# Spreading the first expert's scaling over later groups, with six matmuls of zeros at the start

## The chip, the cores and the metric

The kernel runs on one core of a Trainium2 chip. A core has five engines that run their own instruction streams and meet at semaphores: TensorE (PE, matmuls; its weight loads are shown apart as PEld), VectorE (DVE), ScalarE (ACT), GpSimd (POOL) and SyncE (SP, which only issues DMA transfers here). SBUF is the working memory; matmuls write to PSUM, which has eight banks of 512 fp32 numbers on each of 128 partitions. The metric is the device time of one execution in microseconds, the median over several runs.

## The reference

Attention with feature maps on 8 batches x 8 heads of 576 x 64 gives x of 4608 x 512; behind it stands a mixture of eight experts whose routing weights P are balanced by eight rounds of normalization:

```python
kv  = einsum('bhsf,bhsd->bhfd', phi(k), v);  z = phi(k).sum(axis=2)
x   = (phi(q) @ kv) / (phi(q) . z + 1e-06)      # as 4608 x 512
P   = exp(x @ w_gate - max)                     # 4608 x 8
for _ in range(8):
    P /= P.sum(1, keepdims=True) + 1e-09
    P /= P.sum(0, keepdims=True) + 1e-09
    P *= N / E
for e in range(8):
    h = maximum(x @ w1[e], 0.0)                 # 512 -> 1024
    out += P[:, e:e + 1] * (h @ w2[e])          # 1024 -> 512
```

## The kernel before

The attention stage fills xT, a bf16 copy of x with the feature dimension on the partitions. The tokens stand in nine groups of 512 (g = 0 to 8), and each group has an fp32 accumulator acc[g] of 128 x 4 x 512 in SBUF.

Expert 0 starts while the routing weights are still being formed. Its second products (`down0`) are therefore copied from PSUM to acc[g] without P, by ScalarE (L795) and VectorE (L802) in turn, and P[:, 0] is put on later: at the head of each group's work for expert 1, `down7` lets ScalarE multiply acc[g] in place, in four instructions of 128 x 512 (L1240). That makes 36 of these scalings.

Experts 1 to 7 use a scheme with seven products instead of eight on half-size blocks. `up7` forms a group's hidden values: TensorE adds products up in a bank (x1 to x4 in bank x, one after another), ScalarE copies intermediate states of it to fp32 buffers U (L1106, `keep`), VectorE adds them to other banks and clips at zero (L1110), and ScalarE writes the last state with a relu (L1115). x2 goes into the bank that x1 wrote, so TensorE can go on there only when ScalarE has copied it; the same holds for x3 and x4. `down7` forms sums S of hidden blocks on VectorE (L986) and the seven products X1 to X4, Y1, Z1, Z2. Their states go to acc[g] in two ways: VectorE multiplies by P and adds (L1218), or ScalarE multiplies by P into a buffer V (L1230) and GpSimd adds V to acc[g] (L1233). There are four U buffers and two V buffers. The second products of a group are interleaved with the first products of the next by a list of names (`ORDER`); the first group of expert 1 has none to be interleaved with.

The code doesn't fix the engines' order itself. Each operation is entered in a `Plan` with an engine, a duration that the code supposes, and keys it reads and writes. `schedule` then takes, again and again, the operation that can start first by these durations (of those that can start together, the one entered first), and the program is written out in that order. A key orders operations in the plan alone. On the chip an instruction waits at semaphores only for the data that it reads or overwrites, and for its place in its engine's queue. A scaling is entered with the planner's duration of 512/1200 + 0.09 = 0.52 us.

At the start, SP loads the first keys and queries into accumulators that aren't in use yet, TensorE transposes them (L545), VectorE and ScalarE copy the transposes (L549, L553), and TensorE multiplies by the feature weights wphi2 (L468), which VectorE has cleared (L818) and filled from two loads (L820).

Of the kernel before, what the change touches and what calls it, by code (L numbers as in the profile page):

```python
# [228 lines left out]
def kernel(  # L229
# [11 lines left out]
    nc = tc.nc  # L241
# [26 lines left out]
    xT = const.tile([128, NP, N], BF16, name="xT")  # L268
    L = const.tile([128, NT, E], FP32, name="L")
    P = const.tile([128, NT, E], FP32, name="P")  # L270

    NA = 5
    acc = [accp.tile([128, 4, DD], FP32, name=f"acc{g}", tag=f"acc{g}") for g in range(NA)]
# [17 lines left out]
    def pe(cols, fn, r=(), w=(), takes=()):  # L291
        plan.op("PE", max(cols / 2400.0 + 0.0025, 0.032), 0.32, fn, r, w, takes)

    def act(el, fn, r=(), w=()):
        plan.op("ACT", el / 1200.0 + 0.09, 0.22, fn, r, w)

    def dve(el, fn, r=(), w=(), shared=False):
        plan.op("DVE", el / 960.0 + 0.09, 0.22, fn, r, w, shared=shared)
# [4 lines left out]
    def dma(queue, nbytes, rate, fn, r=(), w=()):  # L303

        plan.op(queue, 0.8 if queue == "POOL" else 0.6, 0.0, fn, r, w, (), nbytes / rate / (125 / 100))
# [45 lines left out]
    def new(tag):  # L351
        return banks.new(int(tag[1])) if tag in ("P1", "P2") else R[tag].new()
# [29 lines left out]
    def load_qk(b, hh, nh, t, r=()):  # L382

        o = hh % 4
        keys = [o // 2] if nh == 2 else [0, 1]
        if b < 2:
            g = t["f"]
            for x, src in ((1, k), (0, q)):
                i = 2 * x + o // 2
                dma("SP", nh << 17, 268, lambda x=x, src=src, i=i: nc.sync.dma_start(  # L390
                    out=acc[g][:, i:i + nh // 2].rearrange("p a (h c) -> p (a h) c", h=2),
                    in_=src[b, hh:hh + nh, 0:SM].rearrange("h (p j) d -> p h (j d)", j=NJ)),
                    r, [("acc", g, 2 * x + n) for n in keys])
            return
        for x, src in ((1, k), (0, q)):
            dma("POOL", nh << 17, 200, lambda x=x, src=src: nc.gpsimd.dma_start(
                out=t["qk"]()[:, x, o:o + nh],
                in_=src[b, hh:hh + nh, 0:SM].rearrange("h (p j) d -> p h (j d)", j=NJ)),
                r, [(t["qk"], x, i) for i in keys])
# [25 lines left out]
    def new_half(b, i):  # L425

        t = {"T": new("qkT"), "v": new("v_m")}
        if b < 2:
            return {"f": 4 - 2 * b - i, **t}
        return {"qk": new("qk"), **t}  # L430
# [36 lines left out]
    def mm(out_, lhsT, rhs, start, stop):  # L467
        nc.tensor.matmul(out_, lhsT=lhsT, rhs=rhs, start=start, stop=stop)  # L468
# [310 lines left out]
    def akey(g):  # L779
        return ["late"] * (g >= NA) + ["P"] * (g >= 9)  # L780
# [27 lines left out]
    for b in range(2):  # L808
        for i in range(2):
            halves[b, i] = new_half(b, i)  # L810
    load_qk(0, 0, 2, halves[0, 0])
    for i, (queue, eng) in enumerate((("ACT", nc.scalar), ("POOL", nc.gpsimd))):
        dma(queue, 1 << 15, 100, lambda i=i, eng=eng: eng.dma_start(
            out=wphi_f[64 * i:64 * i + 64, :], in_=w_phi), w=[f"wphi_f{i}"])
# [16 lines left out]
    for i in range(2):  # L831
        for x in range(2):
            dve(300, lambda i=i, x=x: nc.vector.memset(vrd[i][x], 0.0),
                w=[("vrd", i, x, h, *y) for h in range(2) for y in ((), (1,))])
# [338 lines left out]
    def down7(e, g, hT, B7):  # L1173
# [64 lines left out]
        if e == 1 and g < 9:  # L1238
            for ts in range(4):
                act(512, lambda ts=ts: nc.scalar.activation(  # L1240
                    out=acc[g][:, ts, :], in_=acc[g][:, ts, :], func=ACT.Copy, bias=0.0,
                    scale=P[:, 4 * g + ts, 0:1]), ["P", ("acc", g, ts)] + akey(g),
                    [("acc", g, ts, j) for j in range(2)])
        x, y, z = new("P1"), new("P1"), new("P1")

# [38 lines left out]
    for e in range(1, E):  # L1284
        w1, w2 = load_w(e, ["late"])
        if e == 1:
            for g in range(NG):
                sums_x(g)
        A7, B7 = sums_w(e, w1, w2)
        for g in (range(NG) if e < E - 1 else [8, *range(8)]):  # L1290
            X = load_x(g)
            hT = [new("hT") for _ in range(2)]
            un = up7(A7, g, X, hT, ["up0"])
            for n in ORDER:
                if len(n) == 3:
                    un[n[:2], int(n[2])]()
                elif dn is not None:
                    dn[n]()
            if dn is not None:
                dn["out"]()  # L1300
            if e == E - 1 and g == 7:
                down8(e, g, hT, w2)
            else:
                dn = down7(e, g, hT, B7)
# [31 lines left out]
```

## Time and profile before

| | |
|---|---|
| median of 3 runs | 1036.96 us (1035.57 to 1037.59) |
| profiled execution | 1036.16 us, of which the span is 1034.4 us |
| TensorE busy | 1013.8 us (98%), 9476 matmuls |
| VectorE busy | 823.7 us (80%) |
| ScalarE busy | 710.9 us (69%) |
| GpSimd busy | 462.8 us (45%) |
| L1240, the 36 scalings | 24.3 us busy, on the chain of waits with 2% of the span |

Busy time is the union of an engine's instructions. A matmul's row shows its own length, 0.273 us for 256 columns, while the next one starts 0.11 us after it, so the ends overlap. Stages lie in the order of time: attention with expert 0's first groups beside it to about 205 us, expert 0 alone to about 254 us, experts 1 to 7 from there to the end.

### The profile page before, as it was taken

Reading aid. Unit: us, or ns where it says so; the run is one execution under the profiler, and the core shown is the slowest. Engines: PE = TensorE matmul, PEld = TensorE weight load, DVE = VectorE, ACT = ScalarE, POOL = GpSimd, SP = SyncE. Lnnn points to the kernel's source line nnn. Section 1 sums busy time; section 2 is a strip of 40 time slices with the busy share of each in tenths; the row PEclk is TensorE's granted clock in tenths of the full one; section 3 lists DMA queues with packets and bytes.
Section 4 is the critical chain, followed back from the end, with each engine's and each line's share of the span. In section 5 each row is a group of like instructions: output and inputs, shape, how many; then the busy total and the mean of one; then the engine's idle time right before and its main releaser. Section 6 shows DMA issues by size and latency. Waiting matters only on the chain.

```text
span 1034.4 us, 24481 instructions
## 1 busy us (share of the span) xinstructions
PE 1013.8 (98%) x9476; PEld 843.0 (81%) x9512; DVE 823.7 (80%) x1626; ACT 710.9 (69%) x1569; POOL 462.8 (45%) x534
## 2 busy tenths in 40 slices
PE   7899999999999999999999999999999999999998
PEld 5666666645788888888888888888888888888886
DVE  7999998987677788778777787788677877786775
ACT  7999999837966666666666656666666566666653
POOL 5877675400243443434443444434444433334442
PEclk9999999999999999999999999999999999999999
DMA  9998996085311161115211341134111611114333
GB/s 261 175 172 145 174 162 103 2 206 140 83 42 52 46 120 41 42 46 100 73 44 50 82 83 42 42 83 92 33 52 44 131 43 42 42 51 124 123 123 123
DMA packets 105237, 93.93 MB, mean 91 GB/s; under 512 B 45392, under 2 KB 80272, under 8 KB 105120
## 3 DMA queue, kind: packets, MB, share of 16 engines
q1 hardware_dynamic: 71360, 68.44, 24.3%
q0 software_dynamic: 33680, 23.90, 16.5%
q8 instruction: 74, 1.21, 0.5%
q14 instruction: 43, 0.35, 0.1%
q10 hardware_dynamic: 80, 0.03, 0.0%
HBM read 94.98 MB, written 14.16 MB: 106 GB/s over the span
## 4 chain that ended last, share of the span: by engine, by line
PE 92%; ACT 4%; DVE 3%; issue 1%; DMA 0%; DVEq 0%; POOLq 0%
PE P L1078 73%; PE P L468 17%; ACT acc L1240 2%; PE P L667 1%; DVE m L460 1%; ACT k L464 1%; PE P L706 1%; ACT q L464 0%; DMA wphi_f<-in_w_phi_dram 0%; DVE xb L687 0%; ACT U L1106 0%; DVE P L679 0%; PE P L672 0%; DVE S L986 0%; DVE m_r L460 0%
## 5 line engine op out<-in xcount | busy, mean ns | idle before, releaser
L1233 POOL TENSOR_TENSOR acc<-acc,V 128x512 f32<-128x512 f32 x248 | 316.1, 1281 | 440.5 <-ACT V L1230 437.6
L1110 DVE CUSTOM_DVE_ANT_0 hT<-P,U 128x512 bf16<-128x512 f32 x378 | 255.1, 687 | 105.9 <-ACT U L1106 56.7
L1106 ACT COPY U<-P 128x512 f32<-128x512 f32 x378 | 217.9, 590 | 139.0 <-PE P L1078 131.0
L1230 ACT ACTIVATE V<-P 128x256 f32<-128x256 f32 x496 | 205.6, 474 | 124.4 <-PE P L1078 119.2
L1218 DVE SCALAR_TENSOR_TENSOR acc<-P,acc 128x256 f32<-128x256 f32 x372 | 160.0, 478 | 73.7 <-PE P L1078 71.6
L1078 PEld LDWEIGHTS <-w 128*128 128x128 bf16 x2016 | 197.2, 98 | 25.2 <-issue 2.0
L1078 PEld LDWEIGHTS <-S 128*128 128x128 bf16 x1984 | 194.2, 98 | 22.4
L1078 PEld LDWEIGHTS <-T 128*128 128x128 bf16 x1512 | 147.9, 98 | 19.7 <-issue 2.5
L1078 PEld LDWEIGHTS <-hT 128*128 128x128 bf16 x1488 | 145.5, 98 | 17.1 <-DVE hT L1110 0.3
L1078 PE MATMUL P<-X,w 128*128 128x256 bf16 x1008 | 154.9, 273 | 0.4 <-ACT U L1106 0.4
L1078 PE MATMUL P<-xT,w 128*128 128x256 bf16 x1008 | 152.5, 273 | 0.9 <-ACT acc L795 0.5
L1078 PE MATMUL P<-X,T 128*128 128x256 bf16 x1008 | 148.6, 273 | 1.5 <-ACT U L1106 1.5
L1078 PE MATMUL P<-w,hT 128*128 128x256 bf16 x992 | 143.4, 273 | 0.0
L1078 PE MATMUL P<-T,S 128*128 128x256 bf16 x1056 | 136.3, 273 | 0.0
L1078 PE MATMUL P<-w,S 128*128 128x256 bf16 x928 | 126.5, 273 | 0.0
L460 DVE TENSOR_REDUCE m<-P 128x4 f32<-128x512 f32 x128 | 83.7, 679 | 3.4 <-PE P L468 2.1
L593 POOL TENSOR_TENSOR v<-v_m,em 128x512 bf16<-128x512 f32 x64 | 67.0, 1046 | 43.1 <-ACT em L464 39.0
L986 DVE TENSOR_TENSOR S<-hT 128x1024 bf16<-128x1024 bf16 x124 | 83.4, 709 | 0.3 <-ACT hT L1115 0.3
L1115 ACT ACTIVATE hT<-P 128x512 bf16<-128x512 f32 x126 | 74.2, 604 | 12.4 <-PE P L1078 11.9
L468 PE MATMUL P<-w,hT 128*128 128x512 bf16 x303 | 77.1, 379 | 0.9 <-DVE m L460 0.2
L1078 PE MATMUL P<-xT,T 128*128 128x256 bf16 x504 | 76.0, 273 | 0.3
L468 PE MATMUL P<-xT,w 128*128 128x512 bf16 x271 | 71.4, 379 | 1.0 <-ACT q L464 0.3
(95 smaller groups left out, 1096.5 us busy)
## 6 DMA issues: line engine op xcount, KB each, us to landing
X<-xd SPq DMA_DIRECT2D x126, 256.0 KB, 2.6
w<-in_moe_w_dram POOLq DMA_DIRECT2D x14, 1024.0 KB, 10.1
v_m<-in_v_dram SPq DMA_DIRECT2D x14, 512.0 KB, 5.2
out_dram<-acc SPq DMA_DIRECT2D x14, 512.0 KB, 2.7
xd<-S SPq DMA_DIRECT2D x18, 256.0 KB, 2.4
qk<-in_k_dram POOLq DMA_DIRECT2D x12, 256.0 KB, 5.5
qk<-in_q_dram POOLq DMA_DIRECT2D x12, 256.0 KB, 6.5
w<-in_moe_w_dram POOLq DMA_DIRECT2D x8, 256.0 KB, 7.7
```

What stands on the lines that cost most here:

```text
L460: dve(el, lambda: nc.vector.tensor_reduce(out=dst(), in_=src(), axis=AX.X, op=ALU.max, apply_absolute_value=True), r, w)
L468: nc.tensor.matmul(out_, lhsT=lhsT, rhs=rhs, start=start, stop=stop)
L593: pool(512, lambda y=y, em=em: nc.gpsimd.tensor_tensor(out=s["v"][y]()[:, :, 0:D], in0=t["v"]()[:, h0:h0 + 2].rearrange("p a (b c) -> p (a ...
L986: lambda: f.tensor_tensor(out=out_(), in0=x(), in1=y(), op=op), r, w, **kw)
L1078: pe(256, lambda i=i, k=k, z=z: nc.tensor.matmul(bank()[:, 256 * i:256 * i + 256], lhsT=lhs(k, i), rhs=rhs(k), start=first and z, stop=k = ...
L1106: act(512, lambda: nc.scalar.copy(out=u[fp][n]().rearrange("p a b -> p (a b)"), in_=x[fp]()), [x[fp]], [u[fp][n]])
L1110: dve(500, lambda: nc.vector._custom_dve(ADD_SAT, out=out_(fp, i, j), in0=bank[fp]().rearrange("p (a b) -> p a b", a=2), in1=u[fp][n](), s ...
L1115: act(512, lambda: nc.scalar.activation(out=out_(fp, i, j), in_=x[fp]().rearrange("p (a b) -> p a b", a=2), func=ACT.Relu, bias=0.0, scale ...
L1218: dve(330, lambda n=n, ts=ts: nc.vector.scalar_tensor_tensor(out=acc[g][:, ts, 256 * j:256 * j + 256], in0=bank()[:, 256 * n:256 * n + 256 ...
L1230: act(390, lambda n=n: nc.scalar.activation(out=u()[:, n, :], in_=bank()[:, 256 * n:256 * n + 256], func=ACT.Copy, bias=0.0, scale=P[:, 4 ...
L1233: pool(670, lambda: nc.gpsimd.tensor_tensor(out=acc[g][:, 2 * i:2 * i + 2, 256 * j:256 * j + 256], in0=acc[g][:, 2 * i:2 * i + 2, 256 * j: ...
L1240: act(512, lambda ts=ts: nc.scalar.activation(out=acc[g][:, ts, :], in_=acc[g][:, ts, :], func=ACT.Copy, bias=0.0, scale=P[:, 4 * g + ts, ...
```

## The change

Two edits. The first enters, ahead of the first loads of wphi, a clearing of 512 numbers of xT on VectorE and six products of 128 x 512 zeros on TensorE into a PSUM bank that nobody reads. They read nothing but the cleared part of xT, which the attention stage writes over later.

The second adds a key to the scalings of groups 2 to 8: the planner counts such a scaling as ready only when the last entered operation that wrote a part of acc of the group two ahead (the GpSimd add behind Y1) has ended by its times.

```diff
     load_qk(0, 0, 2, halves[0, 0])
+    dve(128, lambda: nc.vector.memset(xT[:, 0, 0:512], 0.0), w=[("xT", 0, 0)])
+    pz = new("P1")
+    for i in range(6):
+        pe(1024, lambda: mm(pz(), xT[:, 0, 0:128], xT[:, 0, 0:512], True, True),
+           [("xT", 0, 0)], [pz])
...
             for ts in range(4):
                 act(512, lambda ts=ts: nc.scalar.activation(
                     out=acc[g][:, ts, :], in_=acc[g][:, ts, :], func=ACT.Copy, bias=0.0,
-                    scale=P[:, 4 * g + ts, 0:1]), ["P", ("acc", g, ts)] + akey(g),
+                    scale=P[:, 4 * g + ts, 0:1]), ["P", ("acc", g, ts)] + akey(g)
+                    + ([("acc", g - 2, 0, 0)] if g >= 2 else []),
                     [("acc", g, ts, j) for j in range(2)])
```

Lines behind the first edit move by five, behind the second by six: L1240 becomes L1245, L1106 L1111, L1115 L1120, L1230 L1235, L820 L825.

The first place is ScalarE's queue where expert 0 ends and expert 1's first group begins. Before, with the waits at semaphores in brackets; acc_77 to acc_81 are acc[0] to acc[4], acc_4252 and up are acc[5] and up:

```order
L795 ACTIVATE acc_4254<-P 128x512 [waits PE_49]
L1240 ACTIVATE acc_78<-acc_78,P 128x512 x3
L1240 ACTIVATE acc_79<-acc_79,P 128x512 x3
L795 ACTIVATE acc_4255<-P 128x512 [waits PE_49]
L1240 ACTIVATE acc_79<-acc_79,P 128x512
L1240 ACTIVATE acc_80<-acc_80,P 128x512 x4
L1240 ACTIVATE acc_81<-acc_81,P 128x512
L795 ACTIVATE acc_4255<-P 128x512 [waits PE_49]
L1106 COPY U<-P 128x512 [waits PE_49,Pool_49]
L1106 COPY U<-P 128x512 [waits PE_49]
L1240 ACTIVATE acc_81<-acc_81,P 128x512
```

The same place of the changed kernel, where acc_4259 and up are acc[5] and up:

```order
L795 ACTIVATE acc_4261<-P 128x512 [waits PE_49]
L1245 ACTIVATE acc_78<-acc_78,P 128x512 x3
L795 ACTIVATE acc_4262<-P 128x512 [waits PE_49] x2
L1111 COPY U<-P 128x512 [waits PE_49,Pool_49]
L1111 COPY U<-P 128x512 [waits PE_49] x3
L1111 COPY U<-P 128x512 [waits DVE_49,PE_49] x2
L1120 ACTIVATE hT<-P 128x2x256 [waits PE_49] x2
L1235 ACTIVATE V<-P 128x256 [waits DVE_49,PE_49]
```

The scalings of acc[2] and up have left this place; behind those of acc[1] ScalarE's queue goes straight to the copies out of PSUM.

The second place is ScalarE's queue some four groups later. Before, it holds no scalings any more:

```order
L1106 COPY U<-P 128x512 [waits DVE_49,PE_49]
L1115 ACTIVATE hT<-P 128x2x256 [waits PE_49]
L1230 ACTIVATE V<-P 128x256 [waits PE_49,Pool_49]
L1230 ACTIVATE V<-P 128x256
L1115 ACTIVATE hT<-P 128x2x256 [waits PE_49]
```

In the changed kernel those of acc[4] stand there:

```order
L1111 COPY U<-P 128x512 [waits DVE_49,PE_49] x2
L1245 ACTIVATE acc_81<-acc_81,P 128x512
L1235 ACTIVATE V<-P 128x256 [waits PE_49,Pool_49]
L1235 ACTIVATE V<-P 128x256
L1120 ACTIVATE hT<-P 128x2x256 [waits PE_49] x2
L1245 ACTIVATE acc_81<-acc_81,P 128x512 x3
L1111 COPY U<-P 128x512 [waits DVE_49,PE_49] x2
```

One scaling has come ahead of the group's last V copies and three stand between its two relus and the next group's first U copies; none of them has a wait of its own.

The third place is VectorE's queue at the start of the program, before:

```order
L818 MEMSET wphi_88 128x128
L833 MEMSET vrd_89 128x520
L833 MEMSET vrd_90 128x520
L833 MEMSET vrd_91 128x520
L833 MEMSET vrd_92 128x520
L835 MEMSET colw 128x128
L820 CAST wphi_88<-wphi_f 64x128 x2
L549 CAST qkT<-P 128x512
```

and in the changed kernel (128x256 are four-byte words, two numbers each):

```order
L812 MEMSET xT 128x256
L823 MEMSET wphi_88 128x128
L838 MEMSET vrd_89 128x520
L838 MEMSET vrd_90 128x520
L838 MEMSET vrd_91 128x520
L838 MEMSET vrd_92 128x520
L840 MEMSET colw 128x128
L825 CAST wphi_88<-wphi_f 64x128 x2
```

One memset has come ahead of all others; what follows it is the same. TensorE's queue begins with the six pairs of a weight load and a matmul on xT and goes on as before up to expert 1.

## The prediction

> **What bounds the kernel now.** I read the page's busy times and its chain of waits first, then the table by stretches of time, then TensorE's own timeline at the stretch where the table shows a loss.
>
> ```profile
> PE 1013.8 (98%) x9476; PEld 843.0 (81%) x9512; DVE 823.7 (80%) x1626; ACT 710.9 (69%) x1569; POOL 462.8 (45%) x534
> PE 92%; ACT 4%; DVE 3%; issue 1%; DMA 0%; DVEq 0%; POOLq 0%
> L1240 ACT ACTIVATE acc<-acc,P x36: 706/740/885, 243.4 to 278.3; 128x512 f32<-128x512 f32 x36
> ```
>
> TensorE is busy for 98% of the span and carries 92% of the chain, so time can only be gained where it stands still. The third line (the scaling line alone: shortest, median and longest in ns, first and last start) says that the 36 scalings which the change spreads out all start within 35 us. The table by stretches shows what that does; its columns are the stretch, its length, then busy time and instructions of TensorE, weight loads, VectorE, ScalarE and GpSimd, the granted clock, and DMA.
>
> ```profile
> 255.00:260.00 5.00, 4.48 (x41) 3.77 (x39) 3.08 (x5) 5.00 (x11) 0.45 (x1) 1.00 0.78 104
> 260.00:265.00 5.00, 4.02 (x31) 2.72 (x29) 3.65 (x6) 5.00 (x11) 0.00 (x0) 1.00 0.95 215
> 265.00:270.00 5.00, 3.50 (x32) 2.83 (x30) 2.99 (x5) 5.00 (x11) 0.65 (x1) 1.00 0.00 1
> 270.00:275.00 5.00, 5.00 (x48) 4.50 (x46) 2.33 (x5) 5.00 (x12) 2.73 (x3) 1.00 0.19 52
> 275.00:280.00 5.00, 5.00 (x48) 4.41 (x47) 4.87 (x10) 5.00 (x10) 1.71 (x2) 1.00 0.22 56
> 300.00:400.00 100.00, 100.00 (x919) 89.62 (x917) 79.14 (x138) 61.95 (x130) 43.38 (x35) 1.00 0.29 67
> ```
>
> From 255 to 270 us ScalarE is busy without a pause and TensorE gets 41, 31 and 32 matmuls into stretches that hold 48 from 270 on. At the steady pace (100 us for 919, 0.109 us each) the 7 + 17 + 16 = 40 missing ones are worth 4.35 us. That is all there is to gain at this place: from 300 to 400 us TensorE is busy for 100.00 of 100 us. Who stops it there is in the timelines, of TensorE and then of ScalarE (start, length, what, and in brackets the idle time before and what ended it):
>
> ```profile
> 256.42 0.60 PE L1078 MATMUL P<-xT,w 128*128 128x256 bf16 x4 [0.52 <-ACT acc L795]
> 261.75 0.60 PE L1078 MATMUL P<-X,w 128*128 128x256 bf16 x4 [0.38 <-ACT U L1106]
> 264.68 0.60 PE L1078 MATMUL P<-xT,w 128*128 128x256 bf16 x4 [0.33 <-DVE hT L1110]
> 267.48 0.60 PE L1078 MATMUL P<-X,T 128*128 128x256 bf16 x4 [1.33 <-ACT U L1106]
> 268.58 0.60 PE L1078 MATMUL P<-X,T 128*128 128x256 bf16 x4 [0.17 <-ACT U L1106]
> ...
> 252.11 3.78 ACT L1240 ACTIVATE acc<-acc,P 128x512 f32<-128x512 f32 x6
> 255.79 0.59 ACT L795 ACTIVATE acc<-P 128x512 f32<-128x512 f32 x1
> 263.15 3.81 ACT L1240 ACTIVATE acc<-acc,P 128x512 f32<-128x512 f32 x6
> 266.82 0.61 ACT L1106 COPY U<-P 128x512 f32<-128x512 f32 x1
> ```
>
> Four of the five waits end with a ScalarE copy out of PSUM (L795, L1106), and the two longest of these copies stand right behind six scalings in a row, 3.78 and 3.81 us long. Those copies are what TensorE needs; the scalings are not needed until GpSimd and VectorE add to the same rows of acc.
>
> **The scaling, part by part.** The order in front of this text shows that from the third group on the scalings leave this place: behind the first eight, ScalarE now goes straight to two L795 copies and six U copies. Twenty-eight scalings move to later groups; their number and size don't change.
>
> What comes back at 255 to 270 us: at most 4.35 us. Not all of it, for the third wait above ends with VectorE, and expert 1's first group has no second products of an earlier group to fill TensorE while its own last sums are formed.
>
> ```profile
> L1110 DVE CUSTOM_DVE_ANT_0 hT<-P,U 128x512 bf16<-128x512 f32 x378 | 255.1, 687 | 105.9 <-ACT U L1106 56.7 <-PE P L1078 47.2
> L1078 PE MATMUL P<-X,w 128*128 128x256 bf16 x1008 | 154.9, 273 | 0.4 <-ACT U L1106 0.4
> ```
>
> The next to be late there is therefore the last product's end and its add, 0.27 + 0.69 = 0.96 us, before the first product that reads hT. I take this as uncovered once: 4.35 - 0.96 = 3.4 us gained. The ends are 4.35 (something fills it) and 1.83 (only what stands behind the second row of six comes back: 1.33 + 0.17 of idle time, and twice the 0.273 - 0.109 = 0.164 us by which a matmul's modelled end hides a stop).
>
> What the 28 scalings cost where they go: per group of 12 us, four scalings of 0.63 us (3.78 / 6) are 2.5 us, and ScalarE's share rises from 62% to about 83%. The nearest row on the good side is 270 to 280 us in the table: ScalarE is full in both stretches, seven of the scalings start there (the row below and four more in ones and twos), and TensorE still gets its 48. The nearest on the bad side is the second row of six, 1.83 us lost, 0.31 per scaling, or 28 x 0.31 = 8.5 us.
>
> ```profile
> 275.95 2.10 ACT L1240 ACTIVATE acc<-acc,P 128x512 f32<-128x512 f32 x3
> ```
>
> After the change no row of scalings that stands behind the first eight is longer than three, so the good row is the nearer one: I take 0. The gate itself costs nothing on the chip. It is an entry of the planner, the scaling reads nothing of the group two ahead, and in the built program these scalings carry no wait on GpSimd. Nothing can queue behind a gate that isn't there; what counts is only where they stand in ScalarE's order. GpSimd's and VectorE's adds to a group's acc wait for its scaling, but in the new order each stands at least four V copies ahead of that group's first. SP's order is the same row for row; GpSimd's has a weight load one add earlier or later in three places.
>
> **The six matmuls of zeros.** These are rows of the start: TensorE's, one of the table by stretches, VectorE's, and two of the chain of waits (start, length, what):
>
> ```profile
> 3.58 2.13 PE L545 MATMUL P<-identf,acc 128*128 128x128 f32 x8 [3.58 <-DMA acc<-in_k_dram]
> 6.15 1.89 PE L468 MATMUL P<-wphi,qkT 128*128 128x256 bf16 x8 [0.43 <-DVE qkT L549]
> 7.83 1.06 PE L468 MATMUL P<-qkT,wphi 128*128 128x512 bf16 x2
> 8.68 1.81 PE L545 MATMUL P<-identf,acc 128*128 128x128 f32 x8
> 12.36 0.61 PE L468 MATMUL P<-wphi,rT 128*128 128x256 bf16 x4 [0.42 <-DVE rT L485]
> 12.80 0.38 PE L468 MATMUL P<-rT,wphi 128*128 128x512 bf16 x1
> ...
> 6.00:10.00 4.00, 3.85 (x17) 2.90 (x18) 2.91 (x6) 3.11 (x9) 0.05 (x1) 1.00 1.18 203
> ...
> 0.83 0.17 DVE L818 MEMSET wphi<- 128x128 uint32 x1 [0.83 <-PEq L1320]
> 1.05 2.14 DVE L833 MEMSET vrd<- 128x520 bf16 x4
> 3.17 0.17 DVE L835 MEMSET colw<- 128x128 f32 x1
> 3.76 0.22 DVE L820 CAST wphi<-wphi_f 64x128 bf16<-64x128 f32 x1 [0.42 <-DMA wphi_f<-in_w_phi_dram]
> 5.14 0.22 DVE L820 CAST wphi<-wphi_f 64x128 bf16<-64x128 f32 x1 [1.16 <-DMA wphi_f<-in_w_phi_dram]
> 5.40 0.69 DVE L549 CAST qkT<-P 128x512 bf16<-128x512 f32 x1
> ...
> 6.15 1.05 PE P L468 x4
> 7.22 2.06 ACT k L464 x4
> ```
>
> The memset of 512 numbers lies between 0.17 us (128 four-byte words) and 0.54 (2.14 / 4, 520 bf16); say 0.3. VectorE's row then ends at 3.6 to 3.9 instead of 3.34 and the first cast waits for its load until 3.76; the second, at 5.14, is the one that counts and isn't moved. The zeros can start at about 1.2. Two 512-column products take 0.85 us here (7.83 to 8.68), so six take 2.55 and end near 3.75, 0.17 us behind the first transpose's old start. Its result isn't read before 5.40, so that too is covered; if it were not, it would cost 0.17.
>
> What they could give is the pace. Eight 256-column products at 6.15 take 1.68 us to issue (0.21 each), four at 12.36 take 0.44 (0.11 each): TensorE starts at half pace, though the clock column gives 1.00 from 6 to 10 us too. If it were at full pace by 6.15, the four products of the chain at 6.15 would end 4 x 0.10 = 0.4 us earlier, and ScalarE, which the chain follows from 7.22 on, with them. In the old run the pace doubled somewhere between the rows at 8.68 and 12.36, at least 2.5 us after the first product and 5 us after the first transpose; in the new one TensorE is nearly always busy from 1.2 to 5.9, but 2.1 us of that are transposes, which by themselves didn't suffice. Between 0.4 and 0 no row decides, so I take the middle, 0.2 us gained.
>
> The Trainium skill, "TensorE: Matmul & The Clock Gate", Part 1, says that the clock is released by a busy stretch of about 3.4 us in a window that runs freely, and its Part 4 that transposes don't count as busy in the same way. By that rule 2.55 us of zeros are too few, the front gives 0 and the sum is 0.2 us higher; the old run, still at half pace 5 us after its first transpose, agrees with the second half of it.
>
> **The sum.** The profiled execution took 1036.16 us (span 1034.4): 1036.16 - 3.4 - 0.2 + 0 = 1032.6. It lies 0.8 below the median of the three runs, 1036.96; the four executions' mean is 1036.57. From that mean, 3.6 us less is 1033.0, which I give for the median after.
>
> **Rivals.**
> - *The start of expert 1 is held by something else as well* (VectorE's sums of the weights, which still waited for a load at 254 us, or its sums of hT). For it: the wait ended by L1110. Against it: VectorE is busy for 9.7 of those 15 us. Then only the 1.83 us come back: 1036.57 - 1.8 = 1034.7. Chance 0.17.
> - *Slower: the spread scalings stall groups 2 to 8.* A scaling that ScalarE takes up just ahead of a U copy makes that copy 0.6 us late, and TensorE waits for it where x3 and x4 follow each other. For it: the planner counts 0.52 us for a scaling that takes 0.63, so a row of three runs 0.3 late. Against it: 270 to 280 us. At the bad row's price 1033.0 + 8.5 = 1041.5; it decides from 3.6 / 28 = 0.13 us per scaling on. Chance 0.08.
> - *The zeros do nothing* (the clock gate's rule): 1036.57 - 3.4 = 1033.2. That is half of my forecast's chance and doesn't change its sign.
> - *The order on the chip makes no difference*, because the copies were late for another reason than the scalings: 1036.6. Against it stand the two rows of six right ahead of them. Chance 0.03.
>
> **How the numbers follow.** My forecast, with or without the clock, has 0.72. Its own best end is 1036.57 - 4.35 - 0.4 = 1031.8; the runs of before lie 1 us around their mean, so the range begins at 1031.2. At the top it takes in the first rival, 1034.7, and the spread of 1.0 above it, 1035.8; beyond lie the slower case, the case without effect and some tails, together under 2 in 10. A change of 0.2% is 2.1 us, about what a measurement of this kernel can tell from none. Faster by more: the forecast less a little for the runs' spread, 0.70. Within 0.2%: the first rival, the last, and that little, 0.22. Slower: 0.08.
>
> **What would show it.** Scalings from about 243 us to beyond 340 us instead of 278; about 46 matmuls in each 5 us between 255 and 270 but for one wait of about 1 us ended by VectorE; TensorE still full from 270 to 400 with ScalarE near 83% there. At the start, six rows ahead of L545, and either 0.21 or 0.11 us between the products at 6.15. The prediction is wrong if waits on U copies appear in groups 2 to 8, or if between 255 and 270 TensorE waits as long as before, with VectorE or a load named.

## The result, and the profile after

| | before | after |
|---|---|---|
| median of 22 runs each | 1037.03 us (1035.57 to 1038.33) | 1034.53 us (1033.76 to 1037.45) |
| after over before | | 0.9979 (95% interval 0.9973 to 0.9986) |
| profiled execution | 1036.16 us (span 1034.4) | 1034.51 us (span 1032.7) |

The changed kernel is 0.21% faster, 2.2 us by the ratio and 2.5 by the medians. I had forecast 1033.0 us, 3.6 below before: the right sign, inside the range, with 1.1 to 1.4 us too much of gain.

First the lines of the page on busy times and on the chain of waits, and the scalings' own line:

```profile
PE 1014.7 (98%) x9518; PEld 842.0 (82%) x9518; DVE 822.5 (80%) x1627; ACT 709.9 (69%) x1569; POOL 464.8 (45%) x534
PE 94%; DVE 3%; ACT 2%; issue 0%; DMA 0%; POOL 0%; DVEq 0%; POOLq 0%
L1245 ACT ACTIVATE acc<-acc,P x36: 706/721/767, 244.0 to 352.2; 128x512 f32<-128x512 f32 x36
```

The scalings now start over 108 us instead of 35, as announced ("to beyond 340 us"). ScalarE's share of the chain fell from 4% to 2%; VectorE's did not fall. The table by stretches of the changed kernel (columns as in the prediction):

```profile
255.00:260.00 5.00, 5.00 (x48) 4.49 (x47) 4.22 (x8) 3.58 (x7) 0.82 (x1) 1.00 0.67 89
260.00:265.00 5.00, 4.07 (x35) 3.02 (x34) 4.33 (x8) 2.46 (x5) 0.00 (x0) 1.00 1.05 223
265.00:270.00 5.00, 5.00 (x49) 4.47 (x47) 2.11 (x4) 3.78 (x8) 2.90 (x3) 1.00 0.02 7
300.00:400.00 100.00, 99.24 (x910) 88.80 (x909) 80.50 (x140) 70.01 (x148) 43.58 (x35) 1.00 0.28 64
350.00:360.00 10.00, 9.24 (x85) 8.13 (x84) 9.91 (x16) 8.16 (x18) 4.51 (x4) 1.00 0.27 59
```

At the start of expert 1, 41, 31 and 32 matmuls have become 48, 35 and 49: the gain is there. But the middle stretch is still short, and between 300 and 400 us, where before all 100.00 us were busy, 0.76 us are now missing, all of them between 350 and 360 us, where VectorE is busy for 9.91 of 10 us. Who stops TensorE is in its timeline, at the start of expert 1 and later:

```profile
261.75 0.39 PE L1083 MATMUL P<-w,hT 128*128 128x256 bf16 x2 [0.24 <-DVE hT L1115]
262.35 0.83 PE L1083 MATMUL P<-w,hT 128*128 128x256 bf16 x6 [0.20 <-DVE hT L1115]
264.11 1.03 PE L1083 MATMUL P<-w,hT 128*128 128x256 bf16 x8 [0.49 <-ACT V L1235]
...
356.22 0.60 PE L1083 MATMUL P<-xT,T 128*128 128x256 bf16 x4 [0.76 <-DVE hT L1115]
```

No wait on a U copy is left, in this group or a later one. The first three waits are those of a group that has no older work beside it: twice a product waits for the sums hT that it reads, once the next one for ScalarE to empty the bank into V. The wait at 356 us is new. What VectorE does ahead of it is in the chain of waits, from the left (start, length, what):

```profile
346.82 1.74 DVE S L991
348.57 1.57 DVE acc L1223 x4
350.14 0.61 DVE S L991
...
351.98 0.68 DVE S L991
352.66 0.60 DVE hT L1115
353.26 0.61 DVE T L991
353.89 1.67 DVE w L991
355.57 0.61 DVE hT L1115
...
356.22 43.83 PE P L1083 x400
```

Two sums of 128 x 1024 (L991) take 1.74 and 1.67 us here, where the median of this line's 304 operations is 0.68 and only four others are over 0.9. The timelines of VectorE and GpSimd at that place show what stands beside them:

```profile
353.18 0.68 DVE L991 TENSOR_TENSOR T<-w 128x1024 bf16<-128x1024 bf16 x1
353.89 1.67 DVE L991 TENSOR_TENSOR w<-w 128x1024 bf16<-128x1024 bf16 x1
355.49 0.68 DVE L1115 CUSTOM_DVE_ANT_0 hT<-P,U 128x512 bf16<-128x512 f32 x1
...
346.75 1.26 POOL L1238 TENSOR_TENSOR acc<-acc,V 128x512 f32<-128x512 f32 x1 [0.52 <-ACT V L1235]
...
353.75 2.94 POOL L1238 TENSOR_TENSOR acc<-acc,V 128x512 f32<-128x512 f32 x2 [5.73 <-ACT V L1235]
```

Each long sum began while a GpSimd add was under way (from 346.75 and from 353.75 us), about 0.1 us behind its start, and ends 0.55 us behind the end of that add, which is 1.26 us long (the last row holds two adds).

To add this up for all kernels I use one measure. Two successive matmuls on the same data start a fixed time apart (0.109 us for 256 columns); what lies between two starts beyond that is TensorE's loss at that place. Lost from 250 to 276 us ("start of expert 1"): 4.64 us before, 1.43 after. Lost after 276 us ("later", single losses over 0.1 us): 0.25 before, at 401.5 us (another gap there, of one product's length at 1023.3 us, I take for a record missing from the trace); 1.19 after, 0.26 at 284.0 and 0.93 at 356.2. And the attention stage, taken at TensorE's last product with w_gate, ended 0.56 us later (206.47 before, 207.03 after). -3.21 + 0.94 + 0.56 = -1.71 us; the spans differ by 1.64.

### The profile page after: what moved, and what is told of

It is laid out like the page before. It is cut to its first block, busy times and chain, and to the rows that moved or that the text cites. A ratio compares the mean times of both kernels' runs of the same rounds, so it can differ in the third digit from the quotient of the medians.

```text
span 1032.7 us, 24533 instructions
## 1 busy us (share of the span) xinstructions
PE 1014.7 (98%) x9518; PEld 842.0 (82%) x9518; DVE 822.5 (80%) x1627; ACT 709.9 (69%) x1569; POOL 464.8 (45%) x534
## 4 chain that ended last, share of the span: by engine, by line
PE 94%; DVE 3%; ACT 2%; issue 0%; DMA 0%; POOL 0%; DVEq 0%; POOLq 0%
PE P L1083 73%; PE P L468 18%; PE P L667 1%; DVE m L460 1%; ACT q L464 1%; ACT k L464 1%; PE P L706 1%; DMA wphi_f<-in_w_phi_dram 0%; DVE S L991 0%; PE P L672 0%; DVE xb L687 0%; DVE hT L1115 0%; DVE P L679 0%; DVE acc L1223 0%; DVE m_r L460 0%
## 5 line engine op out<-in xcount | busy, mean ns | idle before, releaser
L1115 DVE CUSTOM_DVE_ANT_0 hT<-P,U 128x512 bf16<-128x512 f32 x378 | 255.3, 688 | 121.5 <-ACT U L1111 68.6
L1111 ACT COPY U<-P 128x512 f32<-128x512 f32 x378 | 216.4, 587 | 126.8 <-PE P L1083 121.7
L1235 ACT ACTIVATE V<-P 128x256 f32<-128x256 f32 x496 | 205.0, 473 | 131.1 <-PE P L1083 119.6
L991 DVE TENSOR_TENSOR S<-hT 128x1024 bf16<-128x1024 bf16 x124 | 84.2, 711 | 0.0
L1120 ACT ACTIVATE hT<-P 128x512 bf16<-128x512 f32 x126 | 73.0, 600 | 13.1 <-PE P L1083 12.3
L468 PE MATMUL P<-w,hT 128*128 128x512 bf16 x320 | 79.5, 379 | 0.2 <-DVE m L460 0.2
L468 PE MATMUL P<-xT,w 128*128 128x512 bf16 x288 | 74.8, 379 | 0.3 <-ACT q L464 0.3
## 6 DMA issues: line engine op xcount, KB each, us to landing
w<-in_moe_w_dram POOLq DMA_DIRECT2D x14, 1024.0 KB, 10.2
```

The source lines that it names most:

```text
L991: lambda: f.tensor_tensor(out=out_(), in0=x(), in1=y(), op=op), r, w, **kw)
L1111: act(512, lambda: nc.scalar.copy(out=u[fp][n]().rearrange("p a b -> p (a b)"), in_=x[fp]()), [x[fp]], [u[fp][n]])
L1115: dve(500, lambda: nc.vector._custom_dve(ADD_SAT, out=out_(fp, i, j), in0=bank[fp]().rearrange("p (a b) -> p a b", a=2), in1=u[fp][n](), s ...
L1120: act(512, lambda: nc.scalar.activation(out=out_(fp, i, j), in_=x[fp]().rearrange("p (a b) -> p a b", a=2), func=ACT.Relu, bias=0.0, scale ...
L1235: act(390, lambda n=n: nc.scalar.activation(out=u()[:, n, :], in_=bank()[:, 256 * n:256 * n + 256], func=ACT.Copy, bias=0.0, scale=P[:, 4 ...
```

## The experiments

Of the eight further kernels the first four (gate_only to short_adds) ran beside one set of runs of before (median 1036.97 us, 22 runs), the other four beside a second (1036.88 us, 28 runs). This table has the measured times, and the three places in each one's profiled execution, as differences to before; "sum" is their sum, to be set beside the difference of the spans.

| kernel | median us | ratio to before (95%) | end of attention | start of expert 1 | later | sum | spans |
|---|---|---|---|---|---|---|---|
| after | 1034.53 | 0.9979 (0.9973 to 0.9986) | +0.56 | -3.21 | +0.94 | -1.71 | -1.6 |
| gate_only | 1034.89 | 0.9979 (0.9970 to 0.9988) | +0.07 | -3.22 | +0.93 | -2.22 | -2.2 |
| zeros_only | 1036.83 | 1.0000 (0.9991 to 1.0009) | +0.07 | -0.01 | -0.01 | +0.05 | +0.1 |
| no_scaling | 1033.79 | 0.9969 (0.9956 to 0.9981) | +1.01 | -3.22 | -0.25 | -2.46 | -2.5 |
| short_adds | 1033.61 | 0.9969 (0.9958 to 0.9980) | -0.25 | -3.22 | +0.01 | -3.46 | -3.4 |
| half_v | 1035.68 | 0.9991 (0.9982 to 0.9999) | -0.86 | 0.00 | 0.00 | -0.86 | -0.9 |
| half_v_zeros | 1035.66 | 0.9993 (0.9984 to 1.0002) | -1.35 | 0.00 | 0.00 | -1.35 | -1.3 |
| price | 1033.53 | 0.9970 (0.9959 to 0.9982) | +0.26 | -3.21 | +0.01 | -2.94 | -2.9 |
| gate_one | 1034.67 | 0.9981 (0.9972 to 0.9989) | +1.73 | -3.21 | +1.05 | -0.43 | -0.4 |

The sums meet the spans to 0.1 us in every row, so nothing else of any size lies elsewhere. The end of attention differs from -1.35 to +1.73 us between single executions, which is more than most of the effects in question. It follows the landing of one load, as the part on the zeros shows; for the change's own effect the two columns right of it are the sharper reading.

### One part at a time

gate_only has the second edit alone, zeros_only the first alone:

```diff
# gate_only, against before
-                    scale=P[:, 4 * g + ts, 0:1]), ["P", ("acc", g, ts)] + akey(g),
+                    scale=P[:, 4 * g + ts, 0:1]), ["P", ("acc", g, ts)] + akey(g)
+                    + ([("acc", g - 2, 0, 0)] if g >= 2 else []),
# zeros_only, against before
+    dve(128, lambda: nc.vector.memset(xT[:, 0, 0:512], 0.0), w=[("xT", 0, 0)])
+    pz = new("P1")
+    for i in range(6):
+        pe(1024, lambda: mm(pz(), xT[:, 0, 0:128], xT[:, 0, 0:512], True, True),
+           [("xT", 0, 0)], [pz])
```

> The planner's gate on the scalings alone, without the memset and the six matmuls of zeros. My theory: the whole gain is the gate's, so the time lies 2.0 to 2.8 us below before (ratio 0.9973 to 0.9981), TensorE loses about 1.4 us between 255 and 270 us instead of 4.4, and the attention stage ends when it does in before. Rival (the zeros gave part of it): 1.3 to 1.9 us below before. Rival (the zeros cost the 0.55 us by which the attention stage ended later in the changed kernel's profile): about 3 us below before. The products at 6.1 us should stand 0.21 us apart again.

> The memset and the six matmuls of zeros alone, without the gate. My theory: the products at 6.1 us stand 0.11 us apart and ScalarE begins about 0.5 us earlier, but at about 20 us a load of queries lands no earlier than before, so the time is the same within 0.4 us (ratio 0.9996 to 1.0004). Rival (the early start carries through): 0.5 us less, 0.9995. Rival (the zeros cost something): 0.5 us more. The time between 255 and 270 us is as in before, 4.4 us lost.

The gate has the whole gain: 0.9979, the same ratio as both edits together. It has the same new waits too (0.26 us at 283.5 and 0.93 at 355.7). The zeros alone give 1.0000, and the start of expert 1 looks as before in their table by stretches:

```profile
255.00:260.00 5.00, 4.48 (x41) 3.77 (x40) 3.02 (x5) 5.00 (x11) 0.51 (x1) 1.00 0.74 102
260.00:265.00 5.00, 4.03 (x31) 2.72 (x30) 3.59 (x6) 5.00 (x10) 0.00 (x0) 1.00 1.00 217
265.00:270.00 5.00, 3.50 (x32) 2.83 (x30) 3.05 (x5) 5.00 (x11) 0.59 (x1) 1.00 0.00 1
```

### Without the scalings at all

no_scaling is before without the 36 scalings; the first expert's outputs go into the sum without their routing weight.

```diff
-        if e == 1 and g < 9:
+        if e == 1 and g < 0:
```

> The kernel before with the 36 scalings left out: the first expert's outputs are added without their routing weight. It gives the price of all scalings wherever they stand. My theory: the loss at the start of expert 1 falls to the 1.0 to 1.5 us that the first group without second products has by itself, so 3.0 to 3.5 us below before, about 1 us below the changed kernel, whose later waits (0.26 and 0.93 us) fall away. Rival (the wait at 255 to 270 us is all the scalings'): 4.4 us below before. Rival (VectorE or loads hold the start): less than 2 us below.

TensorE's waits from 255 us to the end are these three and no others (its timeline around 262 us):

```profile
262.21 0.39 PE L1078 MATMUL P<-w,hT 128*128 128x256 bf16 x2 [0.24 <-DVE hT L1110]
262.81 0.83 PE L1078 MATMUL P<-w,hT 128*128 128x256 bf16 x6 [0.20 <-DVE hT L1110]
264.56 1.03 PE L1078 MATMUL P<-w,hT 128*128 128x256 bf16 x8 [0.49 <-ACT V L1230]
```

They are the waits of the changed kernel, to 0.01 us each: 1.42 us lost in all. So the scalings' share of the start of expert 1 was 3.2 us, the changed kernel gets all of it back, and the rest belongs to the first group itself. The later waits are gone without the scalings, those of the changed kernel and also the one of before at 401.5 us. The ratio, 0.9969, is the price of the scalings in the order of before; another placing could beat it only by an order that is luckier elsewhere.

### The wait at 356 us

short_adds is the changed kernel with the GpSimd adds of expert 1's group 7 cut to one of 256 columns, so that GpSimd is nearly idle there; that group's outputs are incomplete.

```diff
+            c = 1 if (e, g) == (1, 7) else 256
-                out=acc[g][:, 2 * i:2 * i + 2, 256 * j:256 * j + 256],
-                in0=acc[g][:, 2 * i:2 * i + 2, 256 * j:256 * j + 256], in1=u(), op=ALU.add),
+                out=acc[g][:, 2 * i:2 * i + 2, 256 * j:256 * j + c],
+                in0=acc[g][:, 2 * i:2 * i + 2, 256 * j:256 * j + c], in1=u()[:, :, 0:c],
+                op=ALU.add),
```

> The changed kernel, same order on every engine but for names, with GpSimd's four adds of expert 1, group 7, cut to one column of 256: the rest of these V isn't added. My theory: the 0.93 us that TensorE loses at 356 us come from a VectorE sum of weights that stood 1.67 us long beside these adds; with short adds it is 0.7 us long, TensorE's wait is under 0.2 us, and the time is 0.7 to 1.0 us below the changed kernel. Rival (ScalarE's scalings of group 8 are late and delay U and with it VectorE): the wait stays, the time is that of the changed kernel.

VectorE, GpSimd and TensorE of this kernel at the same place:

```profile
352.37 0.68 DVE L991 TENSOR_TENSOR T<-w 128x1024 bf16<-128x1024 bf16 x1
353.09 0.69 DVE L991 TENSOR_TENSOR w<-w 128x1024 bf16<-128x1024 bf16 x1
353.70 0.68 DVE L1115 CUSTOM_DVE_ANT_0 hT<-P,U 128x512 bf16<-128x512 f32 x1
...
352.94 0.20 POOL L1239 TENSOR_TENSOR acc<-acc,V 128x2 f32<-128x2 f32 x1 [5.73 <-ACT V L1235]
...
354.38 0.27 PE L1083 MATMUL P<-w,hT 128*128 128x256 bf16 x1
354.49 0.60 PE L1083 MATMUL P<-xT,T 128*128 128x256 bf16 x4
```

The sum of the weights takes 0.69 us instead of 1.67, and TensorE goes on at its pace (0.11 us from 354.38 to 354.49) where it stood for 0.76. The order on the engines is the same; only the adds beside the sum are shorter. The cause of the wait at 356 us is thereby shown: the meeting of that sum with a GpSimd add. The sum at 346 us is still long here (1.74 us), and TensorE doesn't wait for it. That one meeting is absorbed is no rule: before has three sums of 1.74 to 1.75 us, and TensorE lost nothing behind those at 373.70 and 422.85 us, but 0.25 us behind the one at 398.15:

```profile
398.15 1.74 DVE S L986
399.90 1.58 DVE acc L1218 x4
401.52 621.54 PE P L1078 x5692
```

The rows of the changed kernel and of short_adds say that the sum waits out the add. The Trainium skill, "SBUF — State Buffer", Who interferes with whom, gives a mechanism that fits it: a VectorE instruction with two SBUF inputs and a GpSimd instruction that reads SBUF share a read port as a lock, and the later one stands until the first is done. The trace agrees (0.68 us alone, 1.67 and 1.74 begun 0.07 to 0.14 us behind an add of 1.26); that it is a port, no run here shows. The rest is in all ten traces: a sum of this shape that began 0.07 to 1.10 us into a whole GpSimd add ended 0.55 or 0.56 us behind that add's end, wherever it began. It goes the other way round too: an add that began 0.02 us into a sum took 1.79 us instead of 1.27.

### A truer duration for the planner

The planner counts a scaling as 0.52 us; the prediction's rows of scalings have 0.63. It also keeps VectorE's sums and GpSimd's adds from overlapping, in its own times. If the meetings come from drift between its times and the chip's, a truer duration should move them. price is the changed kernel with 0.63:

```diff
-                act(512, lambda ts=ts: nc.scalar.activation(
+                act(648, lambda ts=ts: nc.scalar.activation(
```

> The changed kernel with the planner's duration of a scaling raised from 0.52 to 0.63 us, what the trace shows; nothing else is edited, the order comes out anew. My theory: the two late waits (0.26 and 0.93 us) come from VectorE and GpSimd drifting from the plan's times until their operations meet; with the right price they fall under 0.4 us together, and the time is 0.5 to 1.1 us below the changed kernel (ratio to before 0.9966 to 0.9973). Rival (such meetings are chance in any order): one or two waits of 0.2 to 1 us at other places, the time as the changed kernel's.

1033.53 us, 0.9970 (0.9959 to 0.9982): as fast as no_scaling, with the whole computation done. Its table by stretches has TensorE full, and its VectorE timeline has the sum of the weights at its proper length:

```profile
300.00:400.00 100.00, 100.00 (x919) 89.63 (x917) 78.44 (x141) 70.97 (x146) 43.85 (x34) 1.00 0.28 64
...
355.82 0.68 DVE L991 TENSOR_TENSOR w<-w 128x1024 bf16<-128x1024 bf16 x1
```

This version beats before and the changed kernel by the medians; against the changed kernel the intervals overlap, and what tells them apart is the profile (0.93 us lost at 356 us, or nothing). The 0.26 us at 284 us stay in price as in all kernels with a gate; there the next product waits for two VectorE adds out of a bank. No run here changes that alone.

### A gate by one group instead of two

gate_one is price with the key of the group one ahead:

```diff
-                    + ([("acc", g - 2, 0, 0)] if g >= 2 else []),
+                    + ([("acc", g - 1, 0, 0)] if g >= 1 else []),
```

> As the last, and the gate names the group one ahead instead of two, from the second group on; four more scalings leave the start of expert 1. My theory: the loss at 255 to 270 us stays at 1.42 us, since no scaling bounds it any more, and the time is that of the last kernel within 0.5 us, apart from waits by chance meetings of VectorE and GpSimd. Rival (the first eight scalings still cost something there): 0.3 to 0.6 us less.

1034.67 us, 0.9981 (0.9972 to 0.9989). The start of expert 1 is the same to 0.01 us, so the distance of the gate does not matter there. What comes back is new meetings at other places (VectorE at 355 and 483 us, GpSimd at 483 us; then TensorE at two of its four losses):

```profile
355.09 1.64 DVE L991 TENSOR_TENSOR w<-w 128x1024 bf16<-128x1024 bf16 x1
...
482.94 1.75 DVE L991 TENSOR_TENSOR S<-hT 128x1024 bf16<-128x1024 bf16 x1
...
482.87 1.27 POOL L1238 TENSOR_TENSOR acc<-acc,V 128x512 f32<-128x512 f32 x1 [0.52 <-ACT V L1235]
...
357.24 0.49 PE L1083 MATMUL P<-X,w 128*128 128x256 bf16 x3 [0.29 <-ACT U L1111]
...
485.52 0.38 PE L1083 MATMUL P<-xT,w 128*128 128x256 bf16 x2 [0.17 <-DVE acc L1223]
```

TensorE loses 1.30 us behind 276 us, in four places (0.26, 0.46, 0.34, 0.25). The last two, at 485.5 and 511.1 us, each stand behind one long sum and the VectorE adds that came late by it. The 0.46 at 357.2 us ends with a ScalarE copy to U that itself waited for TensorE; whether the long sum at 355 us is its cause stays open. The truer duration alone is therefore no cure: sums over 0.9 us number 10 in before, 6 in the changed kernel, 3 in price and 11 in gate_one. Each new order meets GpSimd at places of its own, and price's order happens to meet it where VectorE has time (one sum of 1.75 us at 407.66, with nothing lost behind it).

### Why the zeros give nothing

The pace did change. These are the first eight products with wphi2 in the timelines of TensorE, first the changed kernel's, with the zeros and the two rows in question around 20 us:

```profile
1.20 2.74 PE L468 MATMUL P<-xT 128*128 128x512 bf16 x6 [1.20 <-DVE xT L812]
...
6.07 1.05 PE L468 MATMUL P<-wphi,qkT 128*128 128x256 bf16 x8 [0.47 <-DVE qkT L549]
...
18.06 1.09 PE L545 MATMUL P<-identf,acc 128*128 128x128 f32 x8 [1.15 <-DMA acc<-in_k_dram]
...
20.59 0.30 PE L545 MATMUL P<-identf,acc 128*128 128x128 f32 x1 [0.86 <-ACT em L464]
```

Eight products take 1.05 us from the first start to the last end, against 1.89 before. With zeros the eight took 1.05 us in four kernels and 1.33 and 1.40 in two (gate_one, short_adds), without them 1.85 to 1.89 in all four others. In 1.05 us the pace is the full one of 0.11 us each. The traces' records of the granted clock agree: the first record of the full clock begins at 4.0 to 6.7 us in the six with zeros and at 7.5 to 10.2 us in the four without. (Before's first record is that of 10.24 us; the clock column shows 1.00 ahead of it as well, and says nothing of the stretch from 6 to 10 us.) So the half of the rule that I had derived from the Trainium skill ("TensorE: Matmul & The Clock Gate", Part 1: about 3.4 us of activity, in a window that runs freely) as "2.55 us of zeros are too few" did not hold: the products run at full pace 4.9 us after the first zero, though the zeros and the transposes are all that lay between. Whether the zeros alone were enough, or the transposes counted beside them, no run here separates.

Nor does the pace always last. In price the granted clock falls back to 0.50 from 10.95 to 14.36 us, behind a stretch from 7.4 us on in which TensorE ran eight transposes and nothing else; four products then take 1.06 us instead of 0.60. In the other five it stayed, and what makes the difference no run shows.

But TensorE stands at 18 and 20 us, and what it waits for are loads of keys and queries. At 20.59 us the view names ScalarE's em instead, which came last by the profile; but the query load landed at 20.45, and in all ten executions this transpose starts 0.135 us after that load has landed. In zeros_only the same transpose starts at 20.10 us, in before at 20.02, and zeros_only's chain of waits goes through the load (last line, from its issue to its landing):

```profile
20.10 0.30 PE L545 MATMUL P<-identf,acc 128*128 128x128 f32 x1 [0.36 <-DMA acc<-in_q_dram]
...
12.12 7.85 DMA acc<-in_q_dram
```

```profile
20.02 0.30 PE L545 MATMUL P<-identf,acc 128*128 128x128 f32 x1 [0.46 <-DMA acc<-in_q_dram]
```

The execution of zeros_only had little lead to lose: its second load of the feature weights landed at 5.67 us instead of 5.12, so ScalarE began on the first products at 7.35 us (7.22 in before), and not the half microsecond sooner that I had expected. The changed kernel had that lead, 6.72 against 7.22, and its transpose still came 0.57 us later than before's, with the load. In this stretch the loads leave no room; the line of before's table by stretches (DMA share before the last number, in GB/s):

```profile
0.00:22.00 22.00, 15.79 (x120) 11.70 (x120) 16.32 (x31) 16.95 (x44) 10.85 (x27) 1.00 0.99 250
```

To see whether the loads take the gain, half_v loads half of the first batch's values only (the other half is set to zero, so the outputs that depend on it are not the reference's), and half_v_zeros is zeros_only with the same edit:

```diff
-        dma("SP", nh << 17, 268, lambda: nc.sync.dma_start(
+        def half():
+            nc.gpsimd.memset(t["v"]()[:, o:o + nh, 128:256], 0.0)
+            nc.sync.dma_start(
+                out=t["v"]()[:, o:o + nh, 0:128],
+                in_=v[b, hh:hh + nh, 0:SM].rearrange("h (p j) d -> p h (j d)", j=NJ)[:, :, 0:128])
+
+        dma("SP", nh << 17, 268, half if b == 0 else lambda: nc.sync.dma_start(
```

> The kernel before with half of the first batch's value loads: 0.5 MB fewer by about 12 us, the other half of these tiles is set to zero by GpSimd. It makes the loads land sooner. My theory (at 20 us TensorE waits for the load of the second batch's queries, whatever came before): these queries land 1 to 2 us sooner, the wait of TensorE at about 20 us that names a load goes or falls under 0.2 us, and the time is 0.3 to 1 us below before. Rival (the loads don't bind there): the attention stage ends as in before and the time is the same within 0.3 us.

> The same lighter loads with the memset and the six matmuls of zeros. My theory: now the early start isn't caught at 20 us, and the kernel is 0.3 to 0.6 us faster than the one with lighter loads alone. Rival (the zeros' gain is lost for another reason, or the clock comes no earlier): the two are the same within 0.2 us.

The lighter loads do move the end of attention: the ratio is 0.9991, and in the profiled execution the query load lands at 18.98 us instead of 19.88. The transpose of around 20 us in half_v and in half_v_zeros:

```profile
19.12 0.30 PE L551 MATMUL P<-identf,acc 128*128 128x128 f32 x1
```

```profile
18.69 0.30 PE L551 MATMUL P<-identf,acc 128*128 128x128 f32 x1
```

Neither row shows a wait, because the modelled ends of the products ahead of it cover one; but both transposes again start 0.135 us after the query load has landed (18.98 and 18.55 us), so the load still releases it. ScalarE is 0.52 us ahead with the zeros (first products taken up at 6.58 against 7.10 us), the load landed 0.43 sooner and the attention stage ended 0.49 sooner (-1.35 against -0.86). This pair alone can't say which of the two moved the end. The medians, 1035.68 and 1035.66, show no gain; I had expected 0.3 to 0.6 us.

The ten traces together can say it. From the landing of this one query load to TensorE's last product with w_gate it takes 186.56 to 186.67 us in every execution, with zeros or without, whether the load landed at 18.55 us (half_v_zeros) or at 21.63 (gate_one). So the load's landing sets the end of attention, and a lead at 7 us counts for nothing unless the load lands sooner. With whole loads it landed at 19.6 to 21.6 us in the five kernels with zeros and at 19.9 to 20.9 in the three without: the zeros don't bring it forward. What makes one execution's load land a microsecond later than another's stays open; with whole loads it was issued at 11.7 to 12.5 us, and the earliest issue (the changed kernel's) was not the earliest landing.

In three pairs of kernels with and without zeros (zeros_only, half_v_zeros, and after against gate_only by their ratios) the difference was never over 0.02% by the ratio.

## Why the prediction was right, and where its sum was off

- *The start of expert 1 comes back but for one bubble* (4.35 - 0.96 = 3.4 us): right in kind. Lost before were 4.64 us by the starts of the matmuls, of which 3.21 came back. The mis-sized term is the bubble: 1.43 us instead of 0.96. I had let the first group wait once, for a last product and its add; it waits twice for hT (0.40 and 0.37 us) and once for the V copy (0.65), as it does without any scalings. The larger loss before makes up for 0.29 of the 0.47 us.
- *Spread out, 28 scalings cost nothing*: this is the step that failed, by 0.94 us. Its reason held: there is no wait on a U copy in any later group, and ScalarE is not late. It was 79% busy from 270 to 352 us, where the scalings now lie, close to the 83% that I had said (70% from 300 to 400, since the last scaling starts at 352). I priced the scalings on the engine that runs them. What they cost lies on another one: they shift the plan's order, and with it where VectorE's sums meet GpSimd's adds, 0.93 us at 356 us. A wait of 0.26 at 284 us came with the gate too; no long sum stands ahead of it, and its cause stays open. Before had such meetings as well, one of which cost 0.25 us at 401.5, and that one went. Before's chain of waits showed the sign, VectorE's sum at 398.15 us, which I didn't follow.
- *The gate costs nothing on the chip*: no row contradicts it; gate_only and gate_one have the same start.
- *The zeros give 0.2 us*: nothing that can be measured. The pace did double in time, which I held for undecided: in four of six kernels ScalarE took up the first products 0.42 us sooner after the second load of the feature weights, the 0.4 of my sum. What failed is that this lead would reach the end; TensorE waits for a query load 12 us later, and its landing sets the end of the stage in all ten traces.
- *The rivals*: "held by something else" (1034.7) is the nearest by its time, but not by its mechanism, which was that only 1.83 us come back at that place; 3.2 did. "Stall groups 2 to 8" (1041.5) has its sign in the 0.94 us, at 0.03 us per scaling against the 0.13 that it needed, but not its mechanism, a late U copy. "The zeros do nothing" is what happened to the time.
- *The sum*: with the terms as measured, -3.21 + 0.94 + 0 = -2.3 us, against a measured 2.2 by the ratio. The misses add up: 0.47 for the bubble less 0.29 for the larger loss, 0.94 for the later groups and 0.2 for the zeros make 1.3 us. That they stayed small is in part luck, since the loss in the later groups goes by where the order happens to meet: 0.26 us in price, 1.30 in gate_one. The range's lower end, 1031.2, doesn't follow from its own terms either: 1031.8 less the runs' 1 us is 1030.8.

## What to carry to other kernels

Work that moves off a busy place is paid for where the order closes again: price it on the engines that share something with it there, not only on the one that runs it. Where two engines' operations must not overlap and only a plan's times keep them apart, a wrong duration of one operation lets them meet; look for operations of one shape whose longest is far above the median, and test a meeting by shortening the other engine's operation. A faster start pays only up to the first load that TensorE must wait for; look for that load before buying the start.

## What the runs showed of the hardware

- A VectorE sum of two SBUF operands, 128 x 1024 bf16, takes 0.68 us alone and 1.64 to 1.75 us when it begins within 0.2 us behind the start of a GpSimd add of 128 x 512 fp32 (1.27 us); it takes 1.54 us when it begins 0.28 behind and 1.00 when 0.82 behind. Begun 0.07 to 1.10 us behind the add's start, it ends 0.55 us after the add's end. It takes 0.69 us beside an add of two columns (0.20 us).
- The other way round, the add takes 1.79 us instead of 1.27 when it begins 0.02 us behind the start of such a sum, and 1.47 when 0.34 behind: it ends 1.13 us after the sum.
- With six products of zeros from 1.2 us on, the first real products ran at 0.11 us for 256 columns in four of six kernels and reached that pace within the first eight in the other two; without zeros it was 0.21. In one of the six the granted clock fell back to 0.50 for 3.41 us at 10.95 us.
- One execution of the same early stage ended up to 2.0 us later than another (206.22 us in short_adds, 208.20 in gate_one), by when one query load landed (19.64 and 21.63). TensorE's transpose starts 0.135 us after that landing in all ten traces.
